# Low parts of exp(-t) in bfloat16, multiplied with 16-bit high parts, in a fused linear-attention and MLP kernel

## The chip, the cores and the metric

The kernel runs on one core of one Trainium2 chip. The metric is the device time of one launch in microseconds (us). The engines that matter here are TensorE (PE in the profile, its weight loads PEld), VectorE (DVE), ScalarE (ACT), GpSimd (POOL) and the DMA queue of SyncE (SP).

## The reference, cut to what matters

```python
batch, n_heads, seq, head_dim = (8, 8, 576, 64); d_feat = 128
def phi(x):
    proj = np.einsum('bhsd,df->bhsf', x, w_phi)
    proj = proj - np.max(np.abs(proj), axis=-1, keepdims=True)
    return np.concatenate([np.exp(proj), np.exp(-proj)], axis=-1)
q_p, k_p = (phi(q), phi(k))
kv = np.einsum('bhsf,bhsd->bhfd', k_p, v)
z = np.sum(k_p, axis=2)
num = np.einsum('bhsf,bhfd->bhsd', q_p, kv)
den = np.einsum('bhsf,bhf->bhs', q_p, z)[..., None] + 1e-06
x = num / den, as 4608 tokens x 512
h = x @ w_in                                  # 512 x 2048
out = (h / (1.0 + np.exp(-1.702 * h))) @ w_out  # 2048 x 512
```

The kernel carries most operands as a high part and a low part, and adds up three products: high by high, high by low, low by high. Both signs of the exponent are needed: exp(t) lies in (0, 1], exp(-t) is at least 1 and has a much wider range.

## The kernel before, in words

**Work.** There are 32 attention units (batch b from 0 to 7, pair of heads hp from 0 to 3), each over 512 rows of two heads. The last 64 rows of each batch are the tail, done for all heads of a batch at once (`attn_tail`). Units 0 to 5 are "exact": they use full float32 sums for the main rows. Units 6 to 31 use the split form, so 26 units. Then the MLP (`moe_chunk`) runs over chunks of 256 or 384 columns for two batches at a time; it has no float32 matmul.

**One split unit.** `project` gives t for k; `features_k` calls `parts`, which makes for both signs, s=0 for exp(t) and s=1 for exp(-t), a high part by ScalarE and a low part by VectorE (`tensor_sub` of the float32 exp and its high part). From batch 1 on, the s=0 parts are float16 (tiles `eh6`, `el6`, printed in the profile as `eh` and `el` too), and the s=1 parts are float32r (`eh`, `el`, 4 bytes per element). Tiles of the tail have the names `ekth`, `ektl` (k) and `eqth`, `eqtl` (q).

Then come the products of k with v, for each head in one PSUM bank, 5 row tiles (the fifth is the tail) times 2 signs. For each of these there are two matmuls with a 128x128 tile of features as weights: the high part by the high and low part of v side by side (132 columns), and the low part by the high part of v (66 columns):

```python
st = [e[:, t] for e in ek[s]] if t < 4 else [e[:, hp] for e in ekt[s]]
vx = vv[s][:, 4 * h + t] if t < 4 else vt[s][:, hp, h]
mm.append((st[0], vx.rearrange("p i d -> p (i d)"), kv[:, s]))
mm.append((st[1], vx[:, 0], kv[:, s, 0:DV]))
```

`vv` is `(v6, vs)`: the same split of v in float16 and in float32r. The sums become `kf` (float32). Its split, `kz6` for s=0 (float16) and `kzs` for s=1 (float32r), is made by ScalarE (high) and GpSimd (low, `tensor_sub`), one sign after the other. The products with q (`numden`, 9 row tiles per unit, the ninth the tail for both heads with twice the columns) have the same form: `st[0]` by both parts of kz, `st[1]` by the high part.

**The order.** Every operation is recorded (`Recorder.record`), given a planned cost and a priority, and `schedule` then writes out a fixed order for each engine. All instructions are issued by L346, so the profile tells them apart by tiles. In the plan, a matmul with 4-byte weights takes 128/1.2 = 107 units of weight load and n/2.4 + 14 to run; with 2-byte weights it is 128/4.6 = 28 and n/2.4 + 3. A matmul starts in the plan no earlier than the start of the one before it plus its own weight load:

```python
s = max(t, o.est, turn + o.load) if e == "tensor" else max(t, o.est)
```

where another ready matmul could start earlier, that one goes first. So matmuls of the MLP (tiles `hb` and `ab`) come to stand between those of attention. Attention of later batches is spread over the MLP of earlier ones.

Of the kernel before, what the change touches and what calls it, by code (L numbers as in the profile page):

```python
# [11 lines left out]
BF16 = mybir.dt.bfloat16  # L12
# [8 lines left out]
P = 128  # L21
D = 64
NF = 128
# [326 lines left out]
def attn_moe_kernel(ctx, tc, q, k, v, w_phi, w_in, w_out, out):  # L350
# [16 lines left out]
    R = Recorder(nc)  # L367

    def buf(name, shape, dt, n, pool=cp, ordered=True):
        return _Buf(  # L370
            [pool.tile(shape, dt, tag=f"{name}{i}", name=f"{name}{i}") for i in range(n)],
            ordered,
        )

    def static(name, shape, dt):
# [5 lines left out]
    NB = dict(  # L381
        kq=2, vn=1, xs=2, xT=2, ks=12, tl=1, t=4, e=2, eh=3, el=2, ekth=1, ektl=1,
        eqth=1, eqtl=1, xf=1, kzs=1, kf=1, lq=2, nf=1, nt=1, xo=1, x=3, th=2, g=2, gh=2,
        gl=2, osb=2, sm=8, rc=2, sc=6,
    )
# [9 lines left out]
        x=([P, 2, NCT, S], F16), th=([P, CH], F32), g=([P, CH], F32),  # L395
# [3 lines left out]
    pools = {  # L399
        nm: buf(nm, sh, dt, NB[nm], ordered=nm not in ("sc",)) for nm, (sh, dt) in shapes.items()  # L400
    }

    for nm in ("eh", "el", "ekth", "ektl", "eqth", "eqtl"):
        pools[nm + "6"] = buf(nm + "6", [P, 512], F16, NB[nm])

    def new(nm):
        return R.tile(pools[nm])
# [4 lines left out]
    def psa():  # L412
        return R.tile(at, whole=True)

    def f32(ap):
        return ap.bitcast(F32)
# [235 lines left out]
    DV = D + 2  # L652
# [2 lines left out]
    pools["vts"] = buf("vts", [P, NHP, 2, 2, DV], F32R, 1)  # L655

    pools["kz6"] = buf("kz6", [P, 2, 2, DV], F16, 1)
    pools["v6"] = buf("v6", [P, 8, 2, DV], F16, 1)
    pools["vt6"] = buf("vt6", [P, NHP, 2, 2, DV], F16, 1)

# [90 lines left out]

    def two(nm, b, spare):

        return new(nm + "6") if b else new(spare), new(nm)

    def parts(b, src, e, hi, lo):

        his, los = two(hi, b, "eh"), two(lo, b, "el")  # L760
        for i, sg in enumerate((1.0, -1.0)):
            R.scalar.activation(e[i], src, AF.Exp, scale=sg)
            R.scalar.activation(his[i], src, AF.Exp, scale=sg)
            h = his[i] if i == 0 and b else f32(his[i])
            R.vector.tensor_sub(los[i], e[i], h)
        return list(zip(his, los))

    def features_k(b, t, exact, hi="eh", lo="el"):

        e = new("e")  # L770
        if exact:
            e4 = e.rearrange("p (a s f) -> p a s f", a=4, s=2)
            R.scalar.activation(e4[:, :, 0], t, AF.Exp)
            R.scalar.activation(e4[:, :, 1], t, AF.Exp, scale=-1.0)
            return e.rearrange("p (a f) -> p a f", a=4)
        e2 = e.rearrange("p (s n) -> p s n", s=2)
        pr = parts(b, t.rearrange("p a f -> p (a f)"), (e2[:, 0], e2[:, 1]), hi, lo)
        return [[x.rearrange("p (a f) -> p a f", a=4) for x in y] for y in pr]
# [50 lines left out]
    def products(first, last, mm):  # L829

        for i, (st, mv, oi) in enumerate(mm):
            R.tensor.matmul(
                oi,
                st,
                mv,
                start=first and i == 0,
                stop=last and i == len(mm) - 1,
                skip_group_check=True,
            )

    def across(src, dst):

        x = new("xs").rearrange("p s i d -> p (s i d)").bitcast(F32)[0:DV]
        R.scalar.copy(x, src)
        tp = psa()[:, 0 : 4 * DV]
        for j in range(4):
            R.tensor.transpose(
                tp[:, j * DV : (j + 1) * DV], x[:, j * P : (j + 1) * P], ident[0:DV, 0:DV]
            )
        if len(dst.t.shape) == 4:  # L850
            R.scalar.copy(dst, tp.rearrange("p (h s d) -> p h s d", h=2, s=2))
        else:
            R.scalar.copy(dst, tp.rearrange("p (j d) -> p j d", j=4))

    def attn_unit(b, hp, nat, tail, nt, x16, exact, bank):
        kq, vn = nat
        ekt, eqt, vt = tail
# [12 lines left out]
        else:  # L870
            vv = (new("v6"), new("vs"))
# [6 lines left out]
        kf = new("kf")  # L878
        if exact:
            kvt = psa()[0:DV]  # L880
            for h in range(2):
                ek = features_k(b, tk[h], True)
                o = kvt[:, 256 * h : 256 * h + 256]
                mm = [(vn[:, 4 * h + t], ek[:, t], o) for t in range(4)]
                for s in range(2):
                    for i, k in ((0, 0), (0, 1), (1, 0)):
                        mm.append(
                            (vt[s][:, hp, h, k], ekt[s][i][:, hp], o[:, s * NF : s * NF + NF])
                        )
                products(True, True, mm)  # L890
            across(kvt, kf.rearrange("p s h d -> p h s d"))
        for h in range(0 if exact else 2):
            ek = features_k(b, tk[h], False)
            kv = psa()[:, 0 : 4 * DV].rearrange("p (s c) -> p s c", s=2)
            mm = []
            for t in range(5):
                for s in range(2):
                    st = [e[:, t] for e in ek[s]] if t < 4 else [e[:, hp] for e in ekt[s]]
                    vx = vv[s][:, 4 * h + t] if t < 4 else vt[s][:, hp, h]
                    mm.append((st[0], vx.rearrange("p i d -> p (i d)"), kv[:, s]))  # L900
                    mm.append((st[1], vx[:, 0], kv[:, s, 0:DV]))
            products(True, True, mm)
            ls = new("ls")
            R.scalar.copy(ls[:, :, 0:D], kv[:, :, DV : DV + D])
            R.vector.tensor_add(kf[:, :, h], kv[:, :, 0:DV], ls)
        kz = new("kzs")
        if b == 0:
            R.scalar.copy(kz[:, :, :, 0], kf)
            R.vector.tensor_sub(kz[:, :, :, 1], kf, f32(kz[:, :, :, 0]))
            kz = [kz[:, s] for s in range(2)]  # L910
        else:
            kz = [new("kz6"), kz[:, 1]]
            for s in range(2):
                R.scalar.copy(kz[s][:, :, 0], kf[:, s])
                R.gpsimd.tensor_sub(
                    kz[s][:, :, 1], kf[:, s], f32(kz[s][:, :, 0]) if s else kz[s][:, :, 0]
                )


        if exact:  # L920
# [7 lines left out]
        def numden(slots, dst):  # L928

            n = sum(1 if isinstance(h, int) else 2 for h, j in slots)  # L930
            nd = psa()[:, 0 : n * parts_ * DV].rearrange(
                "p (j i d) -> p j i d", j=n, i=parts_
            )
            mm = []
            for i, (h, j) in enumerate(slots):
                for s in range(2):
                    if j < 4:
                        st = [e[:, j * P : (j + 1) * P] for e in eqs[h][s]]
                        o, m = nd[:, i].unsqueeze(1), kz[s][:, h : h + 1]
                    else:  # L940
                        st = [e[:, hp * P : (hp + 1) * P] for e in eqt[s]]
                        o, m = nd[:, i : i + 2], kz[s]
                    if exact:
                        mm += [
                            (st[x], m[:, :, y], o[:, :, 0]) for x, y in ((0, 0), (0, 1), (1, 0))
                        ]
                    else:
                        mm.append(
                            (st[0], m.rearrange("p h i d -> p (h i d)"),
                             o.rearrange("p h i d -> p (h i d)"))  # L950
                        )
                        mm.append((st[1], m[:, :, 0], o[:, :, 0]))
            products(True, True, mm)
            if exact:
                R.scalar.copy(dst, nd[:, :, 0])
            else:
                lq = new("lq")[:, 0:n]
                R.scalar.copy(lq, nd[:, :, 1])
                R.vector.tensor_add(dst, nd[:, :, 0], lq)
# [20 lines left out]
        if not exact:  # L980
            numden([(0, 3), (1, 0), (1, 1)], nf[:, 3:6])
            numden([(1, 2), (1, 3)], nf[:, 6:8])
# [150 lines left out]
    def attention(b):  # L1133
# [22 lines left out]
        for hp in range(NHP):  # L1156
            i = 4 * b + hp
            if hp == 0:
                R.part(u, u + (0.27 if b else 0.1))
                tail = attn_tail(b, tl, i + 3 < NEX, bank)  # L1160
            w = v_att(i)
            R.part(w, w + (0.54 if b else 0.2))
            nat = attn_load(b, hp)
            attn_unit(b, hp, nat, tail, nt, x16, i < NEX, bank)
# [69 lines left out]
```

## Time and profile before

| | us |
|---|---|
| median of 3 runs (1107.79 to 1111.3) | 1108.32 |
| the profiled execution, whole | 1108.59 |
| its span, first to last instruction | 1106.8 |
| TensorE busy (matmuls) | 1071.5 (97%) |
| VectorE busy | 857.5 (77%) |
| ScalarE busy | 713.4 (64%) |
| GpSimd busy | 225.9 (20%) |

The mean granted TensorE clock is 0.993 of full speed. A matmul's duration runs from its start to the modelled end of its pipeline, so the durations of neighbours overlap; how fast TensorE really goes is read from the distance between starts.

### The profile page before, as it was taken

What the parts mean: (1) busy time and instruction counts of PE and PEld (TensorE: products, weight loads), DVE (VectorE), ACT (ScalarE), POOL (GpSimd) and SP (SyncE); (2) the same over time, 40 slices, a digit from 0 to 9 for tenths busy, and PEclk for the clock granted to TensorE, in tenths of its full rate; (3) what the DMA queues carried; (4) which work ended last, traced back from release to release, by engine and by line L of the source; (5) the groups of instructions that cost most, each with busy time, mean ns of one, the idle gap of its engine ahead of it and who ended that gap; (6) DMA issues with size and microseconds to landing.
All of it is one profiled execution on the core that took longest, in us unless ns stands there. A gap on an engine that the chain in (4) does not pass through costs nothing.

```text
span 1106.8 us, 22847 instructions
## 1 busy us (share of the span) xinstructions
PE 1071.5 (97%) x8915; PEld 772.9 (70%) x8915; DVE 857.5 (77%) x1775; ACT 713.4 (64%) x1483; POOL 225.9 (20%) x282
## 2 busy tenths in 40 slices
PE   5996999999999999999999999999999999999997
PEld 3664677778866767678876767687876677677653
DVE  5899989999889988797789997897779867432322
ACT  4676687877668666576677776685677766432423
POOL 6555101321122112221132210211122111100000
PEclk9998999999999999999999999999999999999999
DMA  8855134444244332342243532442233220000101
GB/s 270 274 185 143 58 92 98 75 103 96 50 95 105 82 82 49 63 115 49 30 110 79 119 81 49 71 97 58 49 68 64 43 58 11 11 29 1 30 1 29
DMA packets 174252, 87.80 MB, mean 79 GB/s; under 512 B 140224, under 2 KB 164928, under 8 KB 173888
## 3 DMA queue, kind: packets, MB, share of 16 engines
q1 hardware_dynamic: 174144, 86.34, 33.0%
q8 instruction: 70, 1.15, 0.5%
q14 instruction: 38, 0.31, 0.1%
HBM read 54.59 MB, written 9.44 MB: 58 GB/s over the span
## 4 chain that ended last, share of the span: by engine, by line
PE 86%; DVE 5%; ACT 4%; DMA 2%; issue 1%; SPq 1%; POOL 0%; ACTq 0%; DVEq 0%; POOLq 0%
PE ab L346 33%; PE hb L346 31%; PE at L346 21%; DMA xT<-xs 2%; ACT e L346 1%; SPq L346 1%; DVE sm L346 1%; DVE ks L346 1%; ACT eh L346 0%; DVE gl L346 0%; DMA kq<-in_q_dram 0%; DVE t L346 0%; DVE wbuf L346 0%; DVE vs L346 0%; DVE g L346 0%
## 5 line engine op out<-in xcount | busy, mean ns | idle before, releaser
L346 PE MATMUL hb<-x,wbuf 128*128 128x192 f16 (+3 forms) x3264 | 480.4, 281 | 1.4 <-DVE g L346 1.3
L346 PE MATMUL ab<-wbuf,gh 128*128 128x512 f16 x1152 | 342.0, 382 | 3.0 <-ACT gh L346 3.0
L346 PEld LDWEIGHTS <-wbuf 128*128 128x128 f16 x3264 | 279.0, 98 | 73.2 <-issue 2.2
L346 PE MATMUL ab<-wbuf,gl 128*128 128x512 f16 x576 | 195.2, 382 | 0.4 <-DVE gl L346 0.3
L346 ACT ACTIVATE th<-hb,usc 128x384 f32<-128x384 f32 (+1 forms) x208 | 116.1, 558 | 109.0 <-PE hb L346 102.5
L346 DVE SCALAR_TENSOR_TENSOR g<-th,hb 128x384 f32<-128x384 f32 (+1 forms) x208 | 107.4, 517 | 87.1 <-ACT th L346 85.2
L346 DVE TENSOR_TENSOR el<-e,eh 128x512 f16<-128x512 f32 (+1 forms) x210 | 144.8, 703 | 29.6 <-ACT eh L346 22.6
L346 PEld LDWEIGHTS <-gh 128*128 128x128 f16 x1152 | 108.6, 98 | 84.6 <-ACT gh L346 7.3
L346 ACT ACTIVATE gh<-g,al 128x384 f16<-128x384 f32 (+1 forms) x176 | 107.3, 610 | 65.6 <-DVE g L346 64.7
L346 DVE SCALAR_TENSOR_TENSOR gl<-g,al,gh 128x384 f16<-128x384 f32 (+1 forms) x176 | 110.4, 628 | 37.0 <-ACT gh L346 30.4
L346 POOL TENSOR_TENSOR xf<-nf,rc 128x512 f32<-128x512 f32 x28 | 31.5, 1125 | 447.2 <-DVE rc L346 406.6
L346 PE MATMUL at<-ph,xT 128*128 128x128 f16 x944 | 105.4, 222 | 0.5 <-DVE t L346 0.5
L346 ACT ACTIVATE e<-at 128x512 f32<-128x512 f32 x144 | 85.7, 603 | 29.5 <-PE at L346 29.4
L346 DVE TENSOR_REDUCE sm<-at 128x4 f32<-128x512 f32 x126 | 86.1, 683 | 16.7 <-PE at L346 16.2
L346 ACT ACTIVATE e<-t 128x512 f32<-128x512 f32 x144 | 89.3, 638 | 4.2 <-DVE t L346 3.1
L346 DVE SCALAR_TENSOR_TENSOR t<-at,ks,sm 128x512 f32<-128x512 f32 x118 | 87.7, 744 | 1.1
L346 PEld LDWEIGHTS <-gl 128*128 128x128 f16 x576 | 54.9, 98 | 47.4 <-DVE gl L346 5.7
L346 PE MATMUL at<-vs,eh 128*128 128x132 f32 x208 | 80.3, 386 | 0.0
L346 PE MATMUL at<-kzs,eh 128*128 128x132 f32 x216 | 80.2, 376 | 0.0
L346 PEld LDWEIGHTS <-xT 128*128 128x128 f16 x944 | 69.0, 99 | 14.4 <-issue 1.0
L346 PE MATMUL at<-kzs,el 128*128 128x66 f32 (+1 forms) x212 | 73.6, 351 | 0.6 <-DVE el L346 0.6
L346 PE MATMUL at<-vs,el 128*128 128x66 f32 x208 | 73.9, 356 | 0.0
(197 smaller groups left out, 1921.8 us busy)
## 6 DMA issues: line engine op xcount, KB each, us to landing
vn<-in_v_dram SPq DMA_DIRECT2D x64, 128.0 KB, 2.9
kq<-in_k_dram SPq DMA_DIRECT2D x32, 256.0 KB, 3.3
kq<-in_q_dram SPq DMA_DIRECT2D x32, 256.0 KB, 3.2
tl<-in_v_dram SPq DMA_DIRECT2D x18, 384.0 KB, 3.2
x<-in_moe_w_in_dram SPq DMA_DIRECT2D x10, 512.0 KB, 5.9
x<-in_moe_w_out_dram SPq DMA_DIRECT2D x10, 512.0 KB, 5.6
out_dram<-osb SPq DMA_DIRECT2D x38, 128.0 KB, 2.4
out_dram<-osb SPq DMA_DIRECT2D x16, 256.0 KB, 2.5
```

Of the source, the lines that this page charges most:

```text
L346: f(*[g(a) for a in o.args], **{k: g(a) for k, a in o.kw.items()})
```

## The change

From batch 1 on, the low part of exp(-t) is written as bfloat16 (tiles `elb`, `ektlb`, `eqtlb`) instead of float32r. It is multiplied with the float16 high part of v, which is there already for s=0, and, in the products with q, with a bfloat16 copy of the high sum, `kzb`, made by one more GpSimd instruction per unit (28 units of batches 1 to 7). The high part of exp(-t) and its products stay float32r. Batch 0 is as before.

```diff
+    for nm in ("el", "ektl", "eqtl"):
+        pools[nm + "b"] = buf(nm + "b", [P, 512], BF16, NB[nm])
...
+    pools["kzb"] = buf("kzb", [P, 2, DV], BF16, 1)
...
     def two(nm, b, spare):
-        return new(nm + "6") if b else new(spare), new(nm)
+        if b:
+            return new(nm + "6"), new(nm + "b" if spare == "el" else nm)
+        return new(spare), new(nm)
...
-                            (vt[s][:, hp, h, k], ekt[s][i][:, hp], o[:, s * NF : s * NF + NF])
+                            (vt[0 if i else s][:, hp, h, k], ekt[s][i][:, hp],
+                             o[:, s * NF : s * NF + NF])
...
-                    vx = vv[s][:, 4 * h + t] if t < 4 else vt[s][:, hp, h]
-                    mm.append((st[0], vx.rearrange("p i d -> p (i d)"), kv[:, s]))
-                    mm.append((st[1], vx[:, 0], kv[:, s, 0:DV]))
+                    vx = [x[:, 4 * h + t] if t < 4 else x[:, hp, h] for x in (vv if t < 4 else vt)]
+                    mm.append((st[0], vx[s].rearrange("p i d -> p (i d)"), kv[:, s]))
+                    mm.append((st[1], vx[0][:, 0], kv[:, s, 0:DV]))
...
+            kzl = [z[:, :, 0] for z in kz]          # batch 0
...
+            kzl = [kz[0][:, :, 0], new("kzb")]      # batches 1 to 7
+            R.gpsimd.tensor_copy(kzl[1], kf[:, 1])
...
-                        mm.append((st[1], m[:, :, 0], o[:, :, 0]))
+                        mm.append((st[1], ml, o[:, :, 0]))
```

## Rows read from the trace of the kernel before

**Rows 1.** The page, busy time, share and instructions of each engine.
```profile
PE 1071.5 (97%) x8915; PEld 772.9 (70%) x8915; DVE 857.5 (77%) x1775; ACT 713.4 (64%) x1483; POOL 225.9 (20%) x282
```

**Rows 2.** Busy time of the engines by stretch (from:to length, then each engine).
```profile
core 0: us, PE busy (x) PEld busy (x) DVE busy (x) ACT busy (x) POOL busy (x), PEclk, DMA share, GB/s
166.00:952.00 786.00, 779.60 (x7045) 583.48 (x7044) 671.09 (x1423) 550.10 (x1174) 150.25 (x205) 1.00 0.34 72
...
166.00:360.00 194.00, 193.03 (x1904) 148.95 (x1902) 179.97 (x404) 145.78 (x326) 42.24 (x57) 1.00 0.41 89
```

**Rows 3.** The longest wait of TensorE, 166 to 952 us (total, times, longest).
```profile
PE ab L346 <- ACT gh L346: 3.0, 6, 0.8
```

**Rows 4.** TensorE by form: count, busy us, mean ns of one.
```profile
L346 PE MATMUL at<-vs,el 128*128 128x66 f32 x208 | 73.9, 356 | 0.0
L346 PE MATMUL at<-kzs,el 128*128 128x66 f32 x208 | 72.4, 352 | 0.6 <-DVE el L346 0.6
...
L346 PE MATMUL at<-v,el 128*128 128x66 f16 x208 | 39.7, 194 | 0.0
```

**Rows 5.** Timeline of TensorE around 420 and 439 us (start, us, instruction, count).
```profile
420.22 1.46 PE L346 MATMUL ab<-wbuf,gh 128*128 128x512 f16 x6
...
438.99 0.38 PE L346 MATMUL ab<-wbuf,gl 128*128 128x512 f16 x1
439.02 0.41 PE L346 MATMUL at<-vs,eh 128*128 128x132 f32 x1
439.27 0.39 PE L346 MATMUL ab<-wbuf,gh 128*128 128x512 f16 x1
439.31 0.38 PE L346 MATMUL at<-vs,el 128*128 128x66 f32 x1
439.53 0.24 PE L346 MATMUL at<-v,eh 128*128 128x132 f16 x1
439.61 0.19 PE L346 MATMUL at<-v,el 128*128 128x66 f16 x1
...
440.28 0.22 PE L346 MATMUL at<-v,eh 128*128 128x132 f16 x1
```

**Rows 6.** Timeline of TensorE around 188 us.
```profile
188.30 0.38 PE L346 MATMUL ab<-wbuf,gh 128*128 128x512 f16 x1
...
188.58 0.20 PE L346 MATMUL at<-v,el 128*128 128x66 f16 x1
188.62 0.38 PE L346 MATMUL ab<-wbuf,gl 128*128 128x512 f16 x1
```

**Rows 7.** Timeline of TensorE around 255 us, two float32r products in a row.
```profile
255.56 0.24 PE L346 MATMUL at<-kzs,el 128*128 128x66 f32 x1
255.64 0.24 PE L346 MATMUL at<-kz,eh 128*128 128x132 f16 x1
```

**Rows 8.** Weight loads by form.
```profile
L346 PEld LDWEIGHTS <-el 128*128 128x128 f16 x416 | 41.5, 101 | 7.7 <-DVE el L346 1.4
L346 PEld LDWEIGHTS at<-vs,el 128*128 128x128 f32 x208 | 41.4, 199 | 1.3
```

**Rows 9.** VectorE by form, the low parts.
```profile
L346 DVE TENSOR_TENSOR el<-e,eh 128x512 fp32r<-128x512 f32 x106 | 75.2, 710 | 8.1 <-ACT eh L346 6.7 <-PE at L346 1.1 <-ACT th L346 0.3
L346 DVE TENSOR_TENSOR el<-e,eh 128x512 f16<-128x512 f32 x104 | 72.3, 695 | 21.5 <-ACT eh L346 15.9 <-PE at L346 3.7 <-ACT e L346 1.1
```

**Rows 10.** GpSimd by form, then the timelines of GpSimd and TensorE for one unit.
```profile
L346 POOL CAST vt<-vts 64x256 f16<-64x256 f32 x14 | 6.7, 476 | 11.3 <-PE at L346 9.3 <-DVE vts L346 1.9
...
420.19 0.44 POOL L346 TENSOR_TENSOR kzs<-kf,kzs 128x132 fp32r<-128x132 f32 x1
...
426.02 0.22 PE L346 MATMUL at<-kz,eh 128*128 128x132 f16 x1
```

**Rows 11.** Timeline of TensorE: products of 128 columns in bfloat16 and in float16.
```profile
86.09 2.00 PE L346 MATMUL ab<-wbuf,pick 128*9 128x128 bf16 x16
...
428.99 0.62 PE L346 MATMUL at<-ph,xT 128*128 128x128 f16 x8
```

More of the change, by code (lines that the diff above doesn't have):

```diff
@@ L938, in numden @@
                         st = [e[:, j * P : (j + 1) * P] for e in eqs[h][s]]
-                        o, m = nd[:, i].unsqueeze(1), kz[s][:, h : h + 1]
+                        o, m, ml = nd[:, i].unsqueeze(1), kz[s][:, h : h + 1], kzl[s][:, h : h + 1]
                     else:
                         st = [e[:, hp * P : (hp + 1) * P] for e in eqt[s]]
-                        o, m = nd[:, i : i + 2], kz[s]
+                        o, m, ml = nd[:, i : i + 2], kz[s], kzl[s]
                     if exact:
                         mm += [
-                            (st[x], m[:, :, y], o[:, :, 0]) for x, y in ((0, 0), (0, 1), (1, 0))
+                            (st[0], m[:, :, 0], o[:, :, 0]),
+                            (st[0], m[:, :, 1], o[:, :, 0]),
+                            (st[1], ml, o[:, :, 0]),
                         ]
```

## The prediction

> **What bounds the kernel now.** I read the page first: TensorE is busy 97% of the span, VectorE 77%, ScalarE 64%, GpSimd 20% [rows 1]. A busy share of TensorE alone proves little, because durations of pipelined matmuls overlap, so I went on to the stretches. All products that the change touches but a handful lie between 166 and 952 us, where split units run beside the MLP. There TensorE is busy 779.6 of 786 us, VectorE 671.1 (85%) and ScalarE 550.1 (70%); in the first part, 166 to 360 us, VectorE reaches 180.0 of 194 us (93%) [rows 2]. Then the waits: the longest entry of TensorE in those 786 us is 3.0 us in six waits [rows 3]. So TensorE has work ready nearly always, and its time is the sum of the distances between the starts of its matmuls. That is what the reader should look at, in the timeline: not how long a product lasts, but how much later the next one starts because of it.
>
> **The change part by part.**
>
> *How many products change.* Products of k with v: 26 split units x 2 heads x 4 main row tiles = 208 (the count of vs,el), and 26 x 2 = 52 with the tail. Products with q: 26 x 8 = 208 (kzs,el) and 28 with the tail, of twice the columns. The two exact units of batch 1 add 4 [rows 4]. In all 500 low products go from float32r to 16 bits.
>
> *What a low product costs now.* A 512-column product in a run of six adds (1.46 - 0.38)/5 = 0.216 us [rows 5]; 66 columns at the rate of 512/0.216 would be 0.028, 132 columns 0.056. The stretch from 438.99 to 440.28 is twice the same pattern: MLP product, high float32r, MLP product, low float32r, high float16, low float16. It lasts 1.29 us, and four MLP products, four of 132 and four of 66 columns would take 4 x 0.216 + 4 x 0.056 + 4 x 0.028 = 1.20. So a float32r pair, high and low, costs 0.09/2 = 45 ns beyond its columns. Part of this stands at the product after it: the float16 one that starts right behind the low float32r one takes 0.08 us (439.53 to 439.61) instead of 0.056.
>
> *What it costs in 16 bits.* By luck the trace has the sequence of after: an MLP product, a high float32r one, and then at once a 16-bit one of 66 columns. It goes from 188.30 to 188.62 [rows 6], 0.32 us, against 0.216 + 0.056 + 0.028 = 0.300: the high product alone costs 20 ns beyond its columns, its after-effect on the 16-bit one included. So the low one is to blame for 45 - 20 = 25 ns, and that is what goes away. The reading to 10 ns leaves some 12 to 35 ns. I take 23, a little below the middle, as one start read 10 ns off in the stretch of two pairs moves it by 5.
>
> *Where the weight load stays.* A float32r weight load takes 199 ns, a 16-bit one 101 [rows 8]. In the pattern of rows 5 the MLP product in front hides it, so no gain is booked for it. Where the cover is missing, the low product takes 0.08 us from its start to the next (255.56 to 255.64 [rows 7]), against 0.028: 50 ns. That is rare, and it is the upper bound: 500 x 50 = 25 us. The lower bound for a product of the pattern is 500 x 12 = 6 us. The MLP product that stood in front of each low one as its cover isn't saved; it runs elsewhere at its 0.216.
>
> *The sum on TensorE.* 500 x 23 = 11.5 us.
>
> *VectorE.* 118 low parts per launch (104 main, 14 tail) are written as bfloat16. The nearest row is the float16 form, 695 ns against 710 [rows 9]; 118 x 15 ns = 1.8 us less on an engine that doesn't set the end. Were bfloat16 output dearer than float32r the bound is as small on the other side. ScalarE does what it did.
>
> *GpSimd.* 28 copies of 128x132 from float32 to bfloat16 come on top. The nearest row is the cast of 64x256 at 476 ns [rows 10]; with half the columns, 0.25 to 0.48 us each, 7 to 13 us over the launch on an engine with 20% busy. The copy needs only kf, like the two subtractions beside it. If it goes last, it ends 0.5 us after the subtraction that began at 420.19, that is at about 421.1, and the first product with this sum starts at 426.02: 5 us of cover. If it goes first, the subtractions come 0.5 us later and have the same cover. I book nothing; without the cover it would be 28 x 0.48 = 13 us at most. Queued behind it on GpSimd are the split of v and the division of the next unit, neither of which TensorE was waiting for [rows 3].
>
> *Buffers.* The float16 v is now read one product longer, by the low part of exp(-t), and the float32r v one product less. Both are refilled by the same pair of instructions. Nothing.
>
> *The plan.* The order of all engines is written anew, since a low product costs 30.5 instead of 41.5 in the plan and needs 28 of weight load instead of 107. So it no longer needs a cover. I book nothing, and hold 3 us either way for a different order.
>
> *What reaches the end.* TensorE's waits are under 1% of the 786 us, but in 166 to 360 us VectorE has only 7% to spare, and there a faster TensorE may meet it. A quarter of the gain, 194/786, falls there; I let half of that be lost, some 1.4 us. So 11.5 - 1.4 = 10.1. The profiled execution took 1108.6 us (span 1106.8 and 1.8 around it), 0.3 over the median of the runs. 1108.6 - 10.1 = 1098.5 us.
>
> **A rule that speaks against it.** Weight loads might set the pace of small 16-bit products. Eight products of 128 columns, each with a weight load of its own, take 0.62 us together [rows 11], so with the 0.22 that the last one lasts (a float16 product of 132 columns does in rows 5) they follow in (0.62 - 0.22)/7 = 0.057 us each. That is their columns and 3 ns, although a 16-bit load lasts 101 ns [rows 8]. The Trainium skill, "TensorE: Matmul & The Clock Gate", section "Back-to-back issue gap", says that in a real stream of weight load and matmul the sustained spacing is about 81 ns at 128 columns. By it a 16-bit low product would take 81 ns, more than the float32r one in the pattern, and the kernel would come out slower, by an estimate of about 15 us. By that rule the trace does not go: 57 ns here.
>
> **The rivals.**
>
> 1. *The gain is taken back by the other engines.* The 11 us turn into waits for VectorE and ScalarE: the time stays within 0.3% (3.3 us, about what a measurement of this kernel can tell from no change), 1105 to 1109. For it: VectorE's 85% and 93%. Against: TensorE waits 6 us in 786, and all VectorE work of the stretch would fit into 775 us. 0.11.
>
> 2. *bfloat16 runs slower here (other side).* The only bfloat16 products in the trace, of 128 columns, take 2.00 us for sixteen, about 0.12 each, twice the 0.057 of float16 [rows 11]. If the type is the reason, and not that their moving operand is picked out with a stride of four elements, 66 columns take 0.062 us: 34 ns more than assumed, 11 more than the 23 saved. 468 x 11 ns, and 28 tail products at twice the columns with 45 each, come to 6.4 us: 1115. It decides as soon as a bfloat16 product costs over 23 ns beyond its columns. 0.04.
>
> 3. *Weight loads set the pace (other side).* If each 16-bit low product waits for its load of 101 ns, it costs 101 against 0.028 + 0.023 = 51 ns: 500 x 50 = 25 us, 1134. Against it is the 0.057. 0.02.
>
> 4. *The new order is worse.* A batch's attention comes too late for its MLP chunk, and TensorE waits a few us per batch. VectorE's load is what makes it possible; at 3 us in each of five batches, 15 - 10 = 5 us slower, 1113. 0.05.
>
> 5. *Busy time is what counts.* A low float32r product lasts 354 ns in the mean, a float16 one 194 [rows 4]. 500 x 160 ns = 80 us, 1029 us. The overlapping starts of rows 5 speak against it. 0.02.
>
> **How the numbers follow.** The forecast, 4 to 18 us faster, has 0.76. Together with rival 5 that makes faster by over 0.3% 0.78; within 0.3% is rival 1, 0.11; slower are rivals 2 to 4, 0.11. The likeliest time is 1098.5. The low end of the range is 500 x 35 ns = 17.5 us, 1091. The high end reaches into rival 1, to 1106, where the low bound of 6 us loses half to VectorE. Left out are rivals 2 to 5 and the rest of 1, under 2 in 10.
>
> **What would show it.** In the profile after: no el of the form 128x66 f32 for kz or v beyond batch 0, 416 more 16-bit ones with a mean near 194 ns and weight loads near 101; the high float32r product followed at once by a 16-bit one, 0.03 to 0.04 us long; the stretch of split units shorter by 10 us with the same waits of TensorE; 28 GpSimd copies of 0.25 to 0.48 us and no wait of TensorE for them. TensorE's busy time falls by more than the span does, in no fixed ratio. I am wrong if the starts around a bfloat16 low product lie over 50 ns apart, if TensorE's waits grow by several us, or if the saved distance per product is nearer to 10 ns than to 23.

## The result

| | median us | lowest to highest | ratio to before, 95% interval |
|---|---|---|---|
| before (4 runs) | 1108.5 | 1107.79 to 1111.3 | |
| changed (4 runs) | 1097.51 | 1096.47 to 1100.31 | 0.9895 [0.9878, 0.9912] |

The changed kernel is 11.0 us faster; forecast were 10. The profiled execution took 1097.82 us, its span is 1096.0. The page of the changed kernel, busy time by engine, answers to [rows 1]:

```profile
PE 1062.2 (97%) x8915; PEld 733.2 (67%) x8915; DVE 857.8 (78%) x1775; ACT 712.2 (65%) x1483; POOL 242.4 (22%) x310
```

The last split product starts 11 us earlier, at 941.2 instead of 952.5 us. These are the rows by stretch, as in [rows 2]:

```profile
core 0: us, PE busy (x) PEld busy (x) DVE busy (x) ACT busy (x) POOL busy (x), PEclk, DMA share, GB/s
166.00:360.00 194.00, 192.82 (x1942) 142.77 (x1941) 182.58 (x408) 147.01 (x328) 46.62 (x64) 1.00 0.40 87
...
166.00:941.00 775.00, 769.54 (x7045) 543.49 (x7043) 671.13 (x1423) 548.96 (x1174) 168.20 (x232) 1.00 0.34 73
```

The same 7045 matmuls, busy for 769.5 of 775 us, where it was 779.6 of 786. TensorE idles 5.5 us instead of 6.4, its longest entry in the list of waits is 1.1 us ([rows 3]: 3.0), and VectorE has the same work, 671.1 us, in less time.

```profile
PE ab L346 <- DVE gl L346: 1.1, 3, 0.5
```

The new low products, their weight load, VectorE's and GpSimd's instruction for them, by form (answering to [rows 4], [rows 8], [rows 9] and [rows 10]):

```profile
L346 PE MATMUL at<-v,elb 128*128 128x66 f16 x208 | 42.2, 203 | 0.1
L346 PE MATMUL at<-kzb,elb 128*128 128x66 bf16 x208 | 41.3, 202 | 0.0
...
L346 PEld LDWEIGHTS <-elb 128*128 128x128 bf16 x416 | 40.1, 97 | 23.3 <-DVE elb L346 0.9
...
L346 DVE TENSOR_TENSOR elb<-e,eh 128x512 bf16<-128x512 f32 x104 | 74.8, 719 | 6.7 <-ACT eh L346 6.5
...
L346 POOL CAST kzb<-kf 128x132 bf16<-128x132 f32 x28 | 12.6, 450 | 96.8 <-DVE kf L346 41.9 <-ACT kf L346 37.7 <-DVE sm L346 15.9
```

And the timeline of TensorE in the changed kernel, the pattern that answers to [rows 5]:

```profile
433.12 0.38 PE L346 MATMUL ab<-wbuf,gh 128*128 128x512 f16 x1
433.15 0.41 PE L346 MATMUL at<-vs,eh 128*128 128x132 f32 x1
433.40 0.20 PE L346 MATMUL at<-v,elb 128*128 128x66 f16 x1
433.44 0.22 PE L346 MATMUL at<-v,eh 128*128 128x132 f16 x1
433.50 0.38 PE L346 MATMUL ab<-wbuf,gl 128*128 128x512 f16 x1
```

The low product stands at once behind the high one, with no MLP product between. It takes 0.04 us to the next start, and the float16 one behind it 0.06 instead of 0.08 us.

### The profile page after: what moved, and what is told of

Read it like the earlier page. It is cut to its first block, busy times and chain, and to the rows that moved or that the text cites. A ratio compares the mean times of both kernels' runs of the same rounds, so it can differ in the third digit from the quotient of the medians.

```text
span 1096.0 us, 22834 instructions
## 1 busy us (share of the span) xinstructions
PE 1062.2 (97%) x8915; PEld 733.2 (67%) x8915; DVE 857.8 (78%) x1775; ACT 712.2 (65%) x1483; POOL 242.4 (22%) x310
## 4 chain that ended last, share of the span: by engine, by line
PE 78%; DVE 10%; ACT 4%; issue 3%; DMA 2%; POOL 1%; SPq 1%; ACTq 0%; DVEq 0%; POOLq 0%
PE ab L346 31%; PE hb L346 29%; PE at L346 19%; DMA xT<-xs 1%; DVE sm L346 1%; DVE gl L346 1%; ACT e L346 1%; DVE ks L346 1%; DVE g L346 1%; DVE t L346 1%; ACT eh L346 1%; SPq L346 1%; DVE el L346 1%; DVE elb L346 1%; DMA tl<-in_v_dram 1%
## 5 line engine op out<-in xcount | busy, mean ns | idle before, releaser
L346 PE MATMUL hb<-x,wbuf 128*128 128x192 f16 (+3 forms) x3264 | 474.9, 280 | 1.1 <-DVE g L346 1.1
L346 PE MATMUL ab<-wbuf,gh 128*128 128x512 f16 x1152 | 335.8, 380 | 0.8 <-ACT gh L346 0.6
L346 PE MATMUL ab<-wbuf,gl 128*128 128x512 f16 x576 | 192.2, 380 | 1.3 <-DVE gl L346 1.1
L346 PE MATMUL at<-ph,xT 128*128 128x128 f16 x944 | 108.6, 221 | 0.4 <-ACT x L346 0.4
L346 DVE TENSOR_TENSOR el<-e,eh 128x512 f16<-128x512 f32 (+1 forms) x106 | 74.7, 704 | 12.7 <-ACT eh L346 11.1
L346 DVE TENSOR_TENSOR elb<-e,eh 128x512 bf16<-128x512 f32 x104 | 74.8, 719 | 6.7 <-ACT eh L346 6.5
L346 ACT ACTIVATE eh<-t 128x512 fp32r<-128x512 f32 x105 | 66.4, 648 | 0.3 <-DVE t L346 0.2
```

Of the source, the lines that this page charges most:

```text
L346: f(*[g(a) for a in o.args], **{k: g(a) for k, a in o.kw.items()})
```

## The experiments

Two theories were open. A: the gain is what a float32r low product costs TensorE beyond its columns, a price per product. B: the gain is the order, which the plan writes anew because low products no longer need a cover. Times of experiments are compared with the kernel before as timed beside them (median 1108.8 to 1108.9).

**Old prices for the new products.** The price of a matmul in `cost`:

```diff
-            wide = mybir.dt.size(ap[1].dtype) == 4
+            wide = mybir.dt.size(ap[1].dtype) == 4 or (
+                ap[1].dtype == BF16 and ap[1].shape[-1] == 128
+            )
```

> The changed kernel, but the plan prices its bfloat16 low products like float32r ones (weight load 107, run n/2.4 + 14), so that the order is written as for the kernel before. Theory A, the gain is what each float32r low product costs TensorE beyond its columns, whatever the order: 8 to 11 us faster than before, most of the 11 that the whole change gave. Rival B, the gain is the new order, in which low products need no MLP product in front of them: under 4 us faster.

Measured: 1106.47, ratio 0.9974 [0.9963, 0.9984], 2.5 us faster. That is rival B's figure, and theory A in its simple form falls. But the order did not come out as before: the low products now depend on other tiles (`v6`, `kzb`), and only 5017 of 8915 places in TensorE's order hold the same product. So the run mixes both; a ruler further down parts them.

**New prices for the old products.** A mark on the low tiles from batch 1 on makes `wide` false for them.

```diff
+        x = new(nm)
+        x.tl.cheap = bool(b) and spare == "el"
...
-            wide = mybir.dt.size(ap[1].dtype) == 4
+            wide = mybir.dt.size(ap[1].dtype) == 4 and not getattr(
+                getattr(args[1], "tl", None), "cheap", False
+            )
```

> The kernel before, with its float32r low products of exp(-t), but the plan prices them from batch 1 on like 16-bit ones (weight load 28, run n/2.4 + 3), so that the order is written as for the changed kernel. Theory A: no gain; the low products now stand right behind the high ones without cover, and at up to 50 ns each beyond their columns where the load isn't hidden (255 us in the trace of before) it comes out 5 to 15 us slower than before. Rival B, the order makes the gain: 5 to 11 us faster.

Measured: 1118.95, ratio 1.0091 [1.0076, 1.0106], 10 us slower. The order by itself gives nothing to float32r products; rival B falls in its simple form too.

**Only the k side.** `parts` for q goes on with the float32r tile, and `kzl` is the float32r high part.

```diff
-            return new(nm + "6"), new(nm + "b" if spare == "el" else nm)
+            return new(nm + "6"), new(nm + "b" if spare == "el" and not q else nm)
...
-            kzl = [kz[0][:, :, 0], new("kzb")]
-            R.gpsimd.tensor_copy(kzl[1], kf[:, 1])
+            kzl = [z[:, :, 0] for z in kz]
```

> Only the low parts of k and their products with v become 16 bits wide (264 of 500 products); the q side stays float32r, without the extra GpSimd copy. Theory A, a price per product: 264/500 of 11 us, 5.8 us faster. A rival: the gain sits on one side, for example because the products with q end each unit's chain; then this gives under 3 or over 8 us.

Measured: 1104.32, ratio 0.9957 [0.9944, 0.997], 4.6 us faster.

**Only the q side.** The reverse: `and q` in the first line, and `vx[s]`, `vt[s]` as before.

> Only the low parts of q and their products with kv become 16 bits wide (236 of 500 products, 28 of them of 132 columns), with the GpSimd copy; the k side stays float32r. Theory A: 236/500 of 11 us, 5.2 us faster, and the two sides add up to the whole within 1.5 us. Rival, the gain sits on one side: under 3 or over 8 us.

Measured: 1104.97, ratio 0.996 [0.9947, 0.9974], 4.0 us faster. The two sides gain about alike, 8.6 us together against 11.0; the rest, 2.4 us, is 0.9 more than the 1.5 expected, and within what two orders differ by in later runs.

**Nothing but the type, in the order of before.** The plan is made with the operands and prices of before; at issue, a bfloat16 tile and a constant moving operand are put in.

```diff
+        if b and spare == "el":
+            x.tl.dear = True                 # priced as float32r
+            x.tl.alt = half16[nm]            # issued on these bfloat16 tiles
+            x = V(x.tl, (), half16[nm][0])
...
-                    mm.append((st[1], vx[:, 0], kv[:, s, 0:DV]))
+                    mv = fixed(vx[:, 0], F16) if s else vx[:, 0]   # a constant at issue
+                    mm.append((st[1], mv, kv[:, s, 0:DV]))
```

> The plan of the kernel before to the last instruction (its operands, its prices), but each low part of exp(-t) from batch 1 on is written as bfloat16 when issued, and multiplied with a constant 16-bit tile instead of the high part of v or kv; the output lacks those products. It is the kernel before with nothing but the type of the 500 low products changed. Theory A, a price per product (5 ns at its start and 18 at the product behind it in the trace of before, against 0 and 6 or 7 in the first experiment's trace): 500 x 16 ns, 7 to 9 us faster than before. Rival B, in this order the product itself is worth no more than the 2.5 us that the first experiment gave: 1.5 to 4 us faster.

Measured: 1103.61, ratio 0.9956 [0.9944, 0.9968], 5.2 us faster: between the two figures. 8911 of 8915 places hold the same product as before. So the same products can be laid side by side. The first fence is the kernel before, the second this one; both run from an MLP product behind a float32r one to the same later MLP product, with the same five low products between.

```profile
434.82 0.34 PE L346 MATMUL hb<-x,wbuf 128*128 128x384 f16 x1
...
437.82 1.03 PE L346 MATMUL ab<-wbuf,gh 128*128 128x512 f16 x4
```

```profile
435.03 0.34 PE L352 MATMUL hb<-x,wbuf 128*128 128x384 f16 x1
...
437.94 1.03 PE L352 MATMUL ab<-wbuf,gh 128*128 128x512 f16 x4
```

3.00 us became 2.91: 18 ns for each of the five. Here the price is what theory A says; 500 x 18 would be 9 us. Part of what is missing went into waits, as the row of this kernel's stretch and its two longest waits show:

```profile
166.00:947.00 781.00, 772.99 (x7054) 545.42 (x7052) 671.29 (x1424) 550.91 (x1175) 150.97 (x205) 1.00 0.34 73
```

```profile
PE ab L352 <- ACT gh L352: 3.2, 7, 1.0
PE hb L352 <- DVE g L352: 1.7, 3, 1.1
```

TensorE idles 8.0 us of 781, 1.6 more than before. No single wait stands out (the longest was 3.0 us before). The order was written for slower products, so the likely reason is that TensorE now arrives early.

To size both parts over the whole stretch I took the starts of all matmuls from 166 us to the last split product: from each 16-bit product's start to the next 16-bit one, less the columns at the granted clock (PEclk is 1.00 there, the level of 2.4 GHz; 512 columns are 0.213 us, where products of 512 in a row start 0.216 apart). What is left in pieces under 0.1 us is the price of the products; pieces over 0.1 us are waits and groups of float32 products.

| one profiled execution each | pieces under 0.1 us, sum | over 0.1 us, sum |
|---|---|---|
| before | 39.1 | 28.9 |
| type alone, order of before | 31.9 | 30.5 |
| the changed kernel | 31.1 | 26.2 |
| new products, old prices | 31.0 | 35.5 |
| only the k side | 34.9 | 27.7 |
| only the q side | 35.7 | 28.8 |

So the price fell by 7.2 to 8.1 us wherever all low products have 16 bits. 495 of the 500 lie in this stretch, so it is 15 to 16 ns per product, whatever the order. The pieces over 0.1 us grew by 1.6 us in the old order and fell by 2.7 in the new one.

The same ruler settles what the first runs left open. With the old prices for the new products the price fell by as much, 8.1 us, and a worse order took most of it back (its profiled execution, 1108.84 us, is 2.4 over its median). The two sides add up: 4.2 and 3.4 us, 7.6 together. What their sum lacks against the whole change lies in the pieces over 0.1 us.

**The new order with float32r low products.** The same device the other way round:

```diff
-        pools[nm + "b"] = buf(nm + "b", [P, 512], BF16, NB[nm])
+        pools[nm + "b"] = _Buf(pools[nm].aps, True)      # float32r at issue, planned at the 16-bit price
...
-                    mm.append((st[1], vx[0][:, 0], kv[:, s, 0:DV]))
+                    mv = fixed(vx[0][:, 0], F32R) if s else vx[0][:, 0]
+                    mm.append((st[1], mv, kv[:, s, 0:DV]))
```

> The plan of the changed kernel to the last instruction, but each low part of exp(-t) from batch 1 on is written as float32r when issued, and multiplied with a constant float32r tile; the output lacks those products. The low product stands right behind the high one, without cover for its weight load. Theory A: some 400 such pairs at 65 ns beyond their columns against 14 + 12, plus 12 more at the product behind: 500 x 40 to 50 ns, 20 to 25 us slower than the changed kernel, 9 to 14 slower than before. Rival B, the order is what made it faster: under 5 us slower than the changed kernel, so faster than before.

Measured: 1115.82, ratio 1.0059 [1.0047, 1.0071]: 18.3 us slower than the changed kernel, 7.0 slower than before. That is a little less than theory A's 20 to 25, and rival B is out. 8911 of 8915 places are those of the changed kernel. The timeline at the place that the result section shows:

```profile
440.19 0.38 PE L352 MATMUL ab<-wbuf,gh 128*128 128x512 f16 x1
440.23 0.41 PE L352 MATMUL at<-vs,eh 128*128 128x132 f32 x1
440.48 0.25 PE L352 MATMUL at<-fix,el 128*128 128x66 f32 x1
440.56 0.24 PE L352 MATMUL at<-v,eh 128*128 128x132 f16 x1
440.63 0.38 PE L352 MATMUL ab<-wbuf,gl 128*128 128x512 f16 x1
```

0.44 us, where the changed kernel takes 0.38: without a cover a float32r low product costs 60 ns more than a 16-bit one. Over all 500, covered ones among them, it is 18.3 us / 500 = 37 ns. The four corners:

| | order of before | order of after |
|---|---|---|
| low products float32r | 1108.8 | 1115.8 |
| low products 16 bits | 1103.6 | 1097.5 |

The kernels on the left have no GpSimd copy, those on the right have it.

**Another order for each.** One number of the plan moved, in both kernels:

```diff
-_READY = {"tensor": 282.5, ...
+_READY = {"tensor": 290.0, ...
```

> The kernel before, with one number of the plan moved a little: results of TensorE are planned to be ready after 290 instead of 282.5. All work is the same and the order comes out differently. If the order is worth little, within 2 us of before. If orders that the plan holds for equal differ by several us, as the first experiment's trace suggests, it may be 2 to 6 us off on either side.

> The changed kernel with the same small move of the plan, 290 instead of 282.5. Theory A with a small share of the order: 8 to 12 us faster than the kernel before with the same move. If the 11 us of the change hold several us of a lucky order, the difference of these two falls to 4 to 8, or rises above 13.

Measured: 1109.65 (ratio 1.0006 [0.9997, 1.0014]) for the kernel before, 1100.57 (0.9925 [0.9914, 0.9937]) for the changed one. With this pair of orders the change is worth 9.1 us, against 11.0: theory A with a small share of the order. By the ruler above the short pieces fall from 38.6 to 30.7 us and the long ones from 29.6 to 27.9, so the price is the same 7.9 us and the order gives less.

**float16 in place of bfloat16**, in the very order of the changed kernel (all 8915 places):

```diff
-            return new(nm + "6"), new(nm + "b" if spare == "el" else nm)
+            return new(nm + "6"), new(nm + "b").bitcast(F16) if spare == "el" else new(nm)
...
-            R.vector.tensor_sub(los[i], e[i], h)
+            x = e[i]
+            if b and i:
+                x, h = instead(x, e[0]), instead(h, his[0])
+            R.vector.tensor_sub(los[i], x, h)
```

> The plan of the changed kernel to the last instruction, with the low parts of exp(-t) issued as float16 instead of bfloat16, and the copy of the high sum too. So that the numbers stay finite, the low part of exp(t) is written in their place and the sum of exp(t) is copied; the output lacks the low products of exp(-t). In the trace of the changed kernel a float16 product right behind a bfloat16 one takes 7 ns beyond its columns, against 2 behind float16. Theory A, a change of type costs TensorE some 5 ns, of 16-bit types too: about 300 such places, 1.5 to 2.5 us faster than the changed kernel, about 1095 us. Rival: the two 16-bit types cost the same and the 7 ns have another reason: within 1 us of the changed kernel.

Measured: 1099.01, ratio 0.9919 [0.9905, 0.9932]; not faster than the changed kernel (1.5 us over its 1097.51, half a us outside the rival's margin, with intervals that overlap). The theory that a change between the two 16-bit types costs time falls: the float16 product behind still takes 7 to 8 ns beyond its columns (median of 306 places, from the starts). In the changed kernel the same 7 ns stand behind a float16 low product of exp(t) where an MLP product is right in front of it (5 places), and 2.5 where short products of 132, 66 and 132 columns follow each other (22 places). So the 7 ns seem to go with the place and not with the type; what makes them there stays open.

**Low products at the end of each sum.**

```diff
-                    mm.append((st[1], vx[0][:, 0], kv[:, s, 0:DV]))
-            products(True, True, mm)
+                    (late if s else mm).append((st[1], vx[0][:, 0], kv[:, s, 0:DV]))
+            products(True, True, mm + late)
```

> The changed kernel, with all bfloat16 low products moved to the end of their sum, five or three in a row, behind all others. By theory A fewer changes of type: where now every float32r product is followed by a bfloat16 one and that by a float16 one, it would be one such change per sum for the latter: 1 to 2 us faster than the changed kernel, if the order that comes out waits no more. Rival: each float32r product is then followed by a float16 one at the same price, the order is another, and it is within 3 us on either side.

Measured: 1098.46, ratio 0.9916 [0.9903, 0.993], no better than the changed kernel; the rival held.

**The copy alone**, added to the kernel before:

```diff
+            R.gpsimd.tensor_copy(new("kzb"), kf[:, 1])
```

> The kernel before, with the GpSimd copy of the high sum of exp(-t) into a bfloat16 tile that nobody reads, 28 times. If GpSimd's added 12.6 us are hidden, as the prediction says, within 2 us of before (the order of the plan moves a little). If they lie on the chain from the sums of k to the products with q, up to 12 us slower.

Measured: 1111.95, ratio 1.0038 [1.0025, 1.0051], 3.2 us slower. It missed the 2 us. Its stretch, the longest wait of TensorE in it, and the one for GpSimd:

```profile
166.00:956.00 790.00, 781.16 (x7048) 585.78 (x7047) 671.30 (x1424) 552.11 (x1175) 162.59 (x232) 1.00 0.34 72
```

```profile
PE hb L346 <- DVE g L346: 2.8, 2, 2.5
...
PE at L346 <- POOL kz L346: 0.7, 1, 0.7
```

TensorE waits 0.7 us for GpSimd's subtraction and 2.8 for VectorE, and its idle time is 8.8 us against 6.4. The order of this kernel is another one as well; how much of the 3.2 us is the copy's and how much the order's isn't settled. 0.7 is the part of GpSimd that can be seen.

**Prices nearer to the trace.**

```diff
-            return (load, n / 2.4 + (14.0 if wide else 3.0), 1)
+            return (1.5 * load if wide else load, n / 2.4 + (24.0 if wide else 5.0), 1)
```

> The changed kernel, with prices in the plan nearer to what the traces show: a float32r weight load of 160 instead of 107 and n/2.4 + 24 to run, a 16-bit product n/2.4 + 5 instead of + 3. If the waits and missing covers that are left come from wrong prices, 2 to 5 us faster than the changed kernel; if the order is as good as another one, within 3 us on either side.

Measured: 1107.48, ratio 0.9992 [0.9982, 1.0002]: the same work as the changed kernel, and all but 1.3 us of the gain is gone. Both expectations missed. The last row of its stretches (166 to 952 us in four parts) and its two longest waits:

```profile
sum 786.00, PE 775.09 PEld 544.01 DVE 671.66 ACT 549.32 POOL 162.89; mean PE 193.77 PEld 136.00 DVE 167.91 ACT 137.33 POOL 40.72
```

```profile
PE at L346 <- DVE t L346: 2.3, 4, 0.9
PE at L346 <- ACT eqth L346: 1.5, 1, 1.5
```

TensorE idles 10.9 us instead of 5.5, and its two longest waits are for VectorE and ScalarE instructions of attention (`t` and `eqth`). By the ruler above the short pieces are 31.9 us, as with the other orders, and the long ones 32.7 instead of 26.2. So the order lost the gain, not the price. No version beat the changed kernel.

## Why the prediction was right, and where its sum was off

*What bounds the kernel* held. TensorE had work ready nearly always, before and after, and each shortening of its starts in the stretch came out at the end, less what went into waits.

*500 x 23 ns was too high.* By all starts it is 15 to 16 ns, 7.2 to 8.1 us instead of 11.5. By the medians of the starts before, the low float32r product does cost 23 ns beyond its columns: 5 at itself and 18 at the product behind. The step that failed is the comparison with the bare columns: I took off what the high product costs, but booked nothing for what a 16-bit low one costs in the same place. With nothing but the type changed that is 1.5 ns at itself and 7 to 8 at the product behind, 9 together, which leaves 14. The stretch of rows 6 ended where the product behind begins, so it could not show this. 15 to 16 lie in the bounds of 12 to 35 ns. But by the prediction's own sign (wrong if the saving is nearer to 10 ns than to 23, that is under 16.5) this term failed. The upper bound of 50 ns was no bound: where the cover is missing a float32r low product costs 60 ns more than a 16-bit one.

*The plan at nothing, 3 us either way,* was the second term, and it made up for the first: the new order holds 2.7 us less in pieces over 0.1 us. The four corners show why the two belong together. In the old order 16 bits are worth 5.2 us: the price fell by 7.2, and 1.6 of that came back in the long pieces. The order in which low products need no cover is worth 6.1 us, but only to 16-bit products; to float32r ones it costs 7.0.

*1.4 us lost to VectorE* did not show. In 166 to 360 us VectorE went from 93 to 94% busy and TensorE idled 1.2 us instead of 1.0. So the mechanism held, but that 1098.5 came out within 1 us of 1097.5 is luck: three terms were each off, in opposite ways, and other orders of the same products gave up to 1107.5.

*GpSimd.* 28 copies took 12.6 us, within the 7 to 13; in the changed kernel no wait of TensorE names them. That speaks for a hidden copy in that order only; in another the copy alone made one wait of 0.7 us.

*VectorE.* The main bfloat16 low parts take 719 ns, not 695: 0.9 us more over 104, where 15 ns less for each was booked. VectorE's busy time in the stretch stayed at 671.1 us.

*The rivals.* Rival 1 (taken back by waits) holds in part when the order isn't renewed. Rivals 2 and 3 are out: a bfloat16 low product behind a high one takes 11.5 ns beyond its columns (median; rival 2 wanted over 23), the same order with float16 is not faster, and a low one with its own weight load of 97 ns takes 0.04 us from start to start. By the page of the Trainium skill that the prediction weighed ("TensorE: Matmul & The Clock Gate", "Back-to-back issue gap", about 81 ns at 128 columns) a weight load and matmul could not follow at that pace; the trace after goes against that rule as the one before did. Rival 4, a worse order, didn't come, but 0.05 was too little for it: with the same products the plan gave 1097.5, 1098.5, 1100.6, 1106.5 and 1107.5 us when its prices, latencies or sequence were changed. Rival 5 is out: the busy times of the low products fell by some 150 ns each (354 to 203) and the kernel by 11.0 us / 500 = 22.

## What to carry to other kernels

On a TensorE that is always busy, price a product by how much later the next one starts, and price its replacement in the same place with the same ruler, neighbours included. Where a planner writes the order, a cheaper instruction is worth its full price only if the plan knows of it: the change of type gave 5 us in the old order and the whole change 11 in its own. Before a few us are credited to an edit, move one number of the plan that changes no work: here that alone moved the changed kernel by 3 us and the kernel before by 0.8, within noise, and a change of prices moved the changed kernel by 10.

## What the runs showed of the hardware

By the medians of the starts, a float32r product of 132 columns in front of 16-bit ones delays TensorE by some 13 ns at itself and 12 to 14 at the next product; behind one of 66 columns the next 16-bit product takes 18 ns beyond its columns, where 2 is usual (0.08 us for 132 columns instead of 0.06). A float32r product behind another one, without an MLP product to cover its weight load of 191 to 199 ns, takes 0.08 us for 66 columns, and makes the stretch 60 ns longer than a 16-bit one does. bfloat16 weights with a float16 moving operand run at the pace of float16 with float16: 203 and 202 ns long, and 11.5 ns beyond their columns behind a high float32r product in both kernels of the same order.
